# A decode block on one core: the last 20 row chunks of the down projection in seven loads instead of nine

## The chip, the cores and the metric

The kernel runs on one core of one Trainium2 chip. The metric is the device time of one execution in microseconds (us). A core has a matrix engine (PE, with its weight loads shown as PEld), three further engines for element work (DVE, ACT, POOL), and an engine SP that here only issues transfers. The transfers themselves run on 16 DMA engines that all issuers share; loads issued by SP queue up behind one another and are worked off in order.

## The reference

One token for each of 8 sequences goes through an attention block with a cached window and then a gated feed-forward block, all in float32:

```
h  = x + A(layernorm(x))        # q = x@wq; softmax over the last 1024 cached keys; 32 query heads on 4 kv heads; @wo
g  = layernorm(h) @ w_gate      # 1024 x 3584
u  = layernorm(h) @ w_up        # 1024 x 3584
h2 = h + (gelu(g) * u) @ w_down # 3584 x 1024
```

The activations are tiny (8 rows of 1024). The weights and the cache window are about 111 MB, and each byte is used once.

## The kernel before

All weights pass through two buffers in on-chip memory, `wbuf[0]` and `wbuf[1]`, of 64 KB on each of 128 partitions, 8 MB each. Twelve "units" of 8 MB are loaded in turn, unit 2k into buffer 0 and unit 2k+1 into buffer 1: wq, the keys, the values, wo, then gate and up (two units each). Each unit is one load of 128 rows (one row for each partition) of 64 KB. A load into a buffer waits until PE has finished with what lay there before, so SP issues it while the other buffer is still being filled.

PE works a unit off in one call of `half(i, gates)`: eight steps c = 0 to 7 of four matmuls each (each matmul is a group of 32 output partitions by 512 columns, float32, and appears as two records in the trace, so a step is eight records and a whole half 64). Steps 0 to 3 collect in one part of the PSUM tile `sums[i]`, steps 4 to 7 in the other. PE runs a loop of eight turns; a turn does the b half of one unit, a small summing matmul `y` (line 235), eight transposes (line 240) that turn activations into stationary operands, and then the a half of the next unit. A `gate` is a semaphore that PE waits on ahead of a step, and takes down again by the same amount.

The down projection is 28 row chunks of 128 rows by 1024 columns (512 KB each, 4 KB for each partition). Chunks 0 to 7 ride in the last two units, beside gate and up columns. The last 20 chunks are the end of the program:

- chunks 8 to 23 go into buffer 0 as the loads `wd0` ... (sizes in chunks: `PARTS`), issued as soon as PE has finished the last gate unit there. They are worked off by the last call of `half(0, ...)`, two chunks for each step.
- chunks 24, 25 and 26 go into buffer 1 as the loads `we0` ... (sizes: `ENDPARTS`), issued as soon as PE has finished the last up unit. Each is worked off by `chunk(q)`: four matmuls of 256 columns into the PSUM tile `acc` (line 428).
- chunk 27 comes in two column blocks, `wl0` of 160 and `wl1` of 96 columns for each of four groups (`ENDS`), worked off by four matmuls each (line 453).

Between these lies the fold: DVE adds up what the halves left (`d`, lines 422 and 423; the second add waits for the last matmul of the last `half(0)`), and four matmuls with the constant `add2` bring it into `acc` as well. ACT copies `acc` to `most`, DVE adds each column block of chunk 27 to it, and two stores send the result out.

All loads of weights are issued by SP in program order through one helper, line 93, each with a semaphore that reaches 16 when the load has landed. The gates of the last `half(0)`: ahead of step 0 it waits for `wd0` together with a signal of DVE that the stationary operand for steps 0 to 3 stands; ahead of later steps it waits for the later `wd` loads, and for DVE's signal that the operand for steps 4 to 7 stands (`go_later[0]`, line 408). Since the same loop body serves all turns, POOL gives these gates their amounts for the six earlier turns at the start of the program (line 196).

Of the kernel before, what the change touches and what calls it, by code (L numbers as in the profile page):

```python
# [16 lines left out]
QW = D // NQ  # L17
# [9 lines left out]
UNITS = 12  # L27
EARLY = 8
HEAD = 16
PARTS = (8, 4, 2, 2)  # L30
ENDPARTS = (1, 1, 1)
ENDS = (160, 96)
AHEAD = 3


GATE = (17, 16, 16)
TURNS = 9
NO_B = (1, 4)
NO_A = (3,)
# [2 lines left out]
class Flow:  # L42
# [37 lines left out]
    def run(self, engine, make, *waits, mark=True, gives=None):  # L80
        ins = self.start(engine, make, waits)
        if gives is not None:
            ins.then_inc(*gives)
            return None
        if not mark:
            return None
        self.done[engine] += 1
        ins.then_inc(self.own[engine], 1)
        return self.own[engine], self.done[engine]

    def move(self, name, out, src, *waits, engine="sync", sem=None):
        s = self.sem(name) if sem is None else sem
        self.start(engine, lambda e: e.dma_start(out, src), waits).then_inc(s, 16)  # L93
        return s, 16


def decode_block(nc, x, units, dn, tails, ends, outs):

    fl = Flow(nc)
# [4 lines left out]
    def sb(name, *shape):  # L104
        return nc.alloc_sbuf_tensor(name, list(shape), F32).ap()
# [10 lines left out]
    source = sb("source", P, 2 * N)  # L116

    go = [fl.sem("go_a"), fl.sem("go_b")]
    go_later = [fl.sem(f"go_{i}") for i in range(1, len(PARTS))]
    go_turn, go_fold = fl.sem("go_turn"), fl.sem("go_fold")  # L120


# [17 lines left out]
    def half_a(k, h=1):  # L140
        return at_mark["a", k, h]

    def half_b(k, h=1):
        return at_mark["b", k, h]
# [5 lines left out]
    for u in range(UNITS):  # L150
        k, i = divmod(u, 2)
# [4 lines left out]


    q0 = EARLY
    for i, (n, sem) in enumerate(zip(PARTS, (go[0], *go_later))):
        c0 = (q0 - EARLY) * D  # L160
        move(f"wd{i}", wbuf[0][:, c0:c0 + n * D], dn[i], half_a(passes - 2), sem=sem)
        q0 += n
    assert q0 == EARLY + HEAD
    arrived = {}
    c0 = 0
    for i, n in enumerate(ENDPARTS):
        here = move(f"we{i}", wbuf[1][:, c0:c0 + n * D], tails[i], half_b(nb - 1))
# [4 lines left out]
    last = q0  # L172
# [18 lines left out]
    add2 = sb("add2", P, 2, 32)  # L191
# [3 lines left out]
    for i, g in enumerate(go_later):  # L195
        run("gpsimd", lambda e: e.memset(note[:, i:i + 1], 0.0), gives=(g, GATE[i] * (passes - 1)))

# [10 lines left out]
    def take(sem, n):  # L208
        PE.wait_ge(sem, n).then_inc(sem, -n)  # L209

    def mark(ins):
        ins.then_inc(fl.own["tensor"], 1)

    def half(i, gates):
        gates = dict(gates)
        for c in range(NC):
            if c in gates:
                take(*gates[c])
            h = c // (NC // 2)
            for j in range(NQ):  # L220
                s = NQ * c + j
                ins = PE.matmul(  # L222
                    sums[i][32 * j:32 * j + 32, h * N:(h + 1) * N], still[i][:, 32 * s:32 * s + 32],
                    wbuf[i][:, s * N:(s + 1) * N],
                    start=(c % (NC // 2) == 0), stop=(c % (NC // 2) == NC // 2 - 1))
            if c % (NC // 2) == NC // 2 - 1:
                mark(ins)

    with nc.Fori(1, TURNS, engines=[mybir.EngineType.PE], hint_back_edge=True) as i:
        with PE.If(i != NO_B[0]):  # L230
            with PE.If(i != NO_B[1]):
                half(1, [(0, (go[1], 17))])
                take(go_fold, 1)
                for ch in range(2):
                    ins = PE.matmul(turned[0:32, ch * N:(ch + 1) * N], add2[:, ch, :], y_sb,  # L235
                                    start=True, stop=True)
                mark(ins)
        take(go_turn, 1)
        for n in range(NC):
            ins = PE.transpose(turned[:, n * P:(n + 1) * P], source[:, n * P:(n + 1) * P], ident)  # L240
        mark(ins)
        with PE.If(i != NO_A[0]):
            half(0, [(0, (go[0], 17)), *zip((4, 6, 7), zip(go_later, GATE))])
    fl.done["tensor"] = len(seq)


# [174 lines left out]
    d1 = sb("d1", P, N)  # L421
    tok = run("vector", lambda e: e.tensor_add(d1, rest, sums[0][:, 0:N]), tok, half_a(6, 0))
    d1_ok = run("vector", lambda e: e.tensor_add(d1, d1, sums[0][:, N:2 * N]), tok, half_a(6))


    def quarters(lhs, rhs, *waits, start=False, stop=False):
        for j in range(NQ):
            tok = run("tensor", lambda e: e.matmul(
                acc[32 * j:32 * j + 32, 0:QW], lhs(j), rhs(j), start=start, stop=stop),
                *waits, mark=(stop and j == NQ - 1))  # L430
        return tok

    def chunk(q, **flags):
        t, here = arrived[q]
        return quarters(lambda j: at[:, q, :], lambda j: t[:, j * QW:(j + 1) * QW], here, at_ok, **flags)

    chunk(last - 3, start=True)
    quarters(lambda j: add2[:, j // 2, :], lambda j: d1[:, (j % 2) * QW:(j % 2) * QW + QW], d1_ok)
    chunk(last - 2)
    tok = chunk(last - 1, stop=True)  # L440
    most = sb("most", P, QW)
# [9 lines left out]
    for (c0, n, t, here), d_ps in zip(blocks, (fin, sums[1])):  # L451
        for j in range(NQ):
            tok = run("tensor", lambda e: e.matmul(  # L453
                d_ps[32 * j:32 * j + 32, 0:n], at[:, last, :], t[:, j * n:(j + 1) * n],
                start=True, stop=True), here, d1_ok, mark=(j == NQ - 1))
# [100 lines left out]
```

## Time and profile before

| | |
|---|---|
| time, median of 3 runs | 263.91 us (263.86 to 264.18) |
| profiled execution: its own time | 264.18 us |
| its span, first to last instruction | 262.9 us |
| HBM read | 111.18 MB, 423 GB/s over the span |
| share of the span: PE, PEld, DVE, ACT, POOL | 54%, 17%, 17%, 5%, 3% |
| share of 16 DMA engines' span taken by SP's and the stores' packets | 98.4% |
| granted PE clock, mean | 0.79 of full speed |

The span leaves out 1.28 us of the profiled execution's time. Times within the span count from its start. In rows of the timeline the columns are start, duration from the first start to the last end, engine, line, operation, output and input tile, shape and count; in brackets stands how long the engine sat idle before, and what ended that. In rows of windows, the columns are the window, its length, each engine's busy time with its instructions, the granted clock, the DMA share and GB/s. In the windows a packet is counted where it is recorded, so that a window of 1 us can show a DMA share over 1 or zero while 64 KB rows are under way.

### The profile page before, as it was taken

To read this page: it belongs to the slowest core of one execution; us is meant where nothing else is said; L and a number is where in the kernel's file an instruction comes from. 1 tells how busy PE (TensorE), PEld (TensorE's weight loads), DVE (VectorE), ACT (ScalarE), POOL (GpSimd) and SP (SyncE) were. 2 spreads that over 40 slices of the span, in tenths; PEclk is the share of its full clock that TensorE was granted. 3 is DMA by queue.
4 is the path that set the end of the run, shared out by engine and by line. 5 is a ranking of instruction groups with operands and counts; after the bars stand their busy time and mean duration, and the time that the engine had idled before them with its cause. 6 is when DMAs were issued, how large, how long until landed. Compare 5 with 4: busy or idle time off the path is not lost. (4 is left out here: it accounts for less than half of the span.)

```text
span 262.9 us, 2262 instructions
## 1 busy us (share of the span) xinstructions
PE 141.5 (54%) x968; PEld 44.5 (17%) x968; DVE 43.8 (17%) x115; ACT 13.5 (5%) x19; POOL 7.2 (3%) x18
## 2 busy tenths in 40 slices
PE   0025706926807927608908409728509709319985
PEld 0021201211202312102302102122103202002321
DVE  0340200240100140400410100254100300100432
ACT  1000000000030010000000200000300000200000
POOL 5000100100000000100100000000000000000000
PEclk9999975985966965975976956965957957956999
DMA  8997997999799899979979997997997999799996
GB/s 319 484 459 339 479 479 339 459 479 479 319 479 479 349 449 479 479 319 479 479 329 469 479 469 329 479 479 319 479 479 319 479 479 479 319 479 399 400 421 239
DMA packets 3329, 111.33 MB, mean 424 GB/s; under 512 B 504, under 2 KB 760, under 8 KB 1280
## 3 DMA queue, kind: packets, MB, share of 16 engines
q1 hardware_dynamic: 3168, 111.23, 98.4%
q10 hardware_dynamic: 160, 0.08, 0.1%
q8 instruction: 1, 0.02, 0.0%
HBM read 111.18 MB, written 0.13 MB: 423 GB/s over the span
## 5 line engine op out<-in xcount | busy, mean ns | idle before, releaser
L222 PE MATMUL sum<-w,still 128*32 128x512 f32 x832 | 117.2, 726 | 96.3 <-PEq L209 96.3
L222 PEld LDWEIGHTS sum<-w,still 128*32 128x32 f32 x832 | 32.2, 130 | 177.1 <-issue 177.1
L240 PE MATMUL turned<-ident,source 128*128 128x128 f32 x64 | 11.0, 328 | 21.1 <-PEq L209 21.0
L240 PEld LDWEIGHTS turned<-ident,source 128*128 128x128 f32 x64 | 8.7, 167 | 26.4 <-issue 26.4
L235 PE MATMUL turned<-y_sb,add 128*32 128x512 f32 x24 | 11.3, 592 | 0.9 <-PEq L209 0.9
L318 DVE TENSOR_REDUCE nmax<-sum 128x1 f32<-128x1024 f32 x2 | 2.4, 1223 | 28.4 <-PE sum L222 28.4
L393 DVE TENSOR_TENSOR up<-up,sum 128x512 f32<-128x512 f32 (+1 forms) x2 | 1.4, 686 | 34.3 <-PE sum L222 34.3
L289 DVE TENSOR_SCALAR q<-sum 128x512 f32<-128x512 f32 x2 | 1.4, 692 | 25.2 <-PE sum L222 25.2
L274 DVE COPY still<-turned 128x1024 f32<-128x1024 f32 x4 | 4.7, 1219 | 4.2 <-PE turned L240 4.2
L383 DVE TENSOR_TENSOR gate<-gate,sum 128x512 f32<-128x512 f32 (+1 forms) x2 | 1.4, 685 | 23.6 <-PE sum L222 23.6
L345 DVE SCALAR_TENSOR_TENSOR o<-sum,share,o 128x128 f32<-128x128 f32 x12 | 4.2, 351 | 4.2 <-PE sum L222 3.8
L342 DVE TENSOR_SCALAR o<-sum,share 128x128 f32<-128x128 f32 x2 | 0.7, 350 | 24.0 <-PE sum L222 24.0
L320 ACT ACT_TABLE_LOAD x1 | 1.3, 1283 | 60.2 <-DVE nmax L318 60.2
L235 PEld LDWEIGHTS turned<-y_sb,add 128*32 128x32 f32 x24 | 2.6, 110 | 8.7 <-issue 8.7
L349 POOL MEMSET still<- 128x1024 f32 x2 | 1.9, 951 | 76.0 <-PE sum L222 76.0
L362 DVE TENSOR_TENSOR y_sb<-y_sb,sum 128x512 f32<-128x512 f32 x1 | 0.7, 686 | 15.8 <-PE sum L222 15.8
L294 POOL MEMSET still<- 128x1024 f32 x2 | 1.9, 957 | 46.5 <-PE sum L222 46.5
L360 ACT COPY y_sb<-sum 128x512 f32<-128x512 f32 x1 | 0.6, 586 | 50.7 <-PE sum L222 50.7
L320 ACT ACTIVATE source<-sum,nmax 128x1024 f32<-128x1024 f32 x2 | 2.2, 1113 | 17.1 <-PE turned L240 17.1
L361 DVE TENSOR_TENSOR y_sb<-y_sb,sum 128x512 f32<-128x512 f32 x1 | 0.7, 686 | 14.3 <-PE sum L222 14.3
L305 DVE COPY still<-turned 128x16 f32<-128x16 f32 x32 | 2.7, 161 | 2.1 <-PE turned L240 2.1
L382 ACT COPY gate<-sum 128x512 f32<-128x512 f32 (+1 forms) x2 | 1.2, 584 | 30.4 <-PE sum L222 30.4
(61 smaller groups left out, 40.3 us busy)
## 6 DMA issues: line engine op xcount, KB each, us to landing
w<-dn SPq DMA_DIRECT2D x1, 4096.0 KB, 19.8
w<-dn SPq DMA_DIRECT2D x1, 2048.0 KB, 24.3
w<-dn SPq DMA_DIRECT2D x2, 1024.0 KB, 27.3
w<-tails SPq DMA_DIRECT2D x3, 512.0 KB, 12.0
w<-ends SPq DMA_DIRECT2D x1, 320.0 KB, 13.1
w<-units SPq DMA_DIRECT2D x12, 29.4
w<-ends SPq DMA_DIRECT2D x1, 192.0 KB, 13.1
out<-o_fin SPq DMA_DIRECT2D x1, 80.0 KB, 1.6
```

The source lines that it names most:

```text
L222: ins = PE.matmul(sums[i][32 * j:32 * j + 32, h * N:(h + 1) * N], still[i][:, 32 * s:32 * s + 32], wbuf[i][:, s * N:(s + 1) * N], start=(c ...
L235: ins = PE.matmul(turned[0:32, ch * N:(ch + 1) * N], add2[:, ch, :], y_sb, start=True, stop=True)
L240: ins = PE.transpose(turned[:, n * P:(n + 1) * P], source[:, n * P:(n + 1) * P], ident)
L274: run("vector", lambda e: e.tensor_copy(still[i].rearrange("p (c j m) -> p c j m", c=NC, j=NQ), turned.rearrange("p (c m) -> p c m", c=NC) ...
L289: tok = run("vector", lambda e: e.tensor_scalar(q_sb, sums[hf][:, 0:N], scale, None, op0=ALU.mult), done(0, 0))
L294: cleared.append(run("gpsimd", lambda e: e.memset(still[hf], 0.0), done(0)))
L305: run("vector", lambda e: e.tensor_copy(to[:, :, b, s, a, REP * b:REP * b + REP].rearrange("p k (h i) -> p k h i", h=2), frm[:, s, a * HB ...
L318: tok = run("vector", lambda e: e.tensor_reduce(out=nmax, in_=sums[hf], axis=AX.X, op=ALU.max, negate=True), done(1))
L320: p_ok = run("scalar", lambda e: e.activation(source, sums[hf], AF.Exp, bias=nmax, accum_out=tot), tok, at_mark["t", 1 + hf])
L345: tok = run("vector", lambda e: e.scalar_tensor_tensor(out, o3[:, b], share[hf][:, b:b + 1], o_sb, op0=ALU.mult, op1=ALU.add), tok, done(2 ...
L349: cleared[hf] = run("gpsimd", lambda e: e.memset(still[hf], 0.0), done(2))
L383: tok = run("vector", lambda e: e.tensor_add(gate[:rows], gate[:rows], sums[0][:rows, N:2 * N]), tok, half_a(4 + k))
```

## The change

Two tables of sizes change, and with them the loads. Chunks 8 to 23 come as 10, 4 and 2 chunks in three loads instead of 8, 4, 2 and 2 in four. Chunks 24 to 26 come as 2 and 1 chunks in two loads instead of three of one chunk. The two column blocks of chunk 27 are as before. The number of bytes and their order are the same.

The gates of `half(0)` follow: the wait on DVE's signal for steps 4 to 7 stands alone now (amount 1 instead of 17, since no load ends at that step), the second load is waited for ahead of step 5, and the third ahead of step 7. At the end, the fold's four matmuls go ahead of those of chunk 24 and open the accumulation in `acc`.

```diff
-PARTS = (8, 4, 2, 2)
-ENDPARTS = (1, 1, 1)
+PARTS = (10, 4, 2)
+ENDPARTS = (2, 1)
 ENDS = (160, 96)
...
-GATE = (17, 16, 16)
+GATE = (1, 16, 16)
...
-    go_later = [fl.sem(f"go_{i}") for i in range(1, len(PARTS))]
+    go_later = [fl.sem(f"go_{i}") for i in range(len(GATE))]
...
-    for i, (n, sem) in enumerate(zip(PARTS, (go[0], *go_later))):
+    for i, (n, sem) in enumerate(zip(PARTS, (go[0], *go_later[1:]))):
...
-            half(0, [(0, (go[0], 17)), *zip((4, 6, 7), zip(go_later, GATE))])
+            half(0, [(0, (go[0], 17)), *zip((4, 5, 7), zip(go_later, GATE))])
...
-    chunk(last - 3, start=True)
-    quarters(lambda j: add2[:, j // 2, :], lambda j: d1[:, (j % 2) * QW:(j % 2) * QW + QW], d1_ok)
+    quarters(lambda j: add2[:, j // 2, :], lambda j: d1[:, (j % 2) * QW:(j % 2) * QW + QW], d1_ok,
+             start=True)
+    chunk(last - 3)
     chunk(last - 2)
     tok = chunk(last - 1, stop=True)
```

On SP, which issues the loads, the end of the program is this (`dn` is the source of chunks 8 to 23, `tails` of chunks 24 to 26, `ends` of chunk 27; the shape is partitions by float32 elements; `tensor_done` counts PE's finished halves):

```order
-L93 DMA w<-dn 128x8192 [waits tensor_done]
+L93 DMA w<-dn 128x10240 [waits tensor_done]
 L93 DMA w<-dn 128x4096
-L93 DMA w<-dn 128x2048 x2
-L93 DMA w<-tails 128x1024 [waits tensor_done]
-L93 DMA w<-tails 128x1024 x2
+L93 DMA w<-dn 128x2048
+L93 DMA w<-tails 128x2048 [waits tensor_done]
+L93 DMA w<-tails 128x1024
 L93 DMA w<-ends 128x640
 L93 DMA w<-ends 128x384
```

Four loads of `dn` have become three and three of `tails` two; the waits ahead of the first of each are the same.

On PE, in the loop's `half(0)`, a step of four matmuls is what stands between two gates or a multiple of it (`go_a` is the gate of step 0; in the program before `go_1` to `go_3` are the later ones, in the changed one `go_0` to `go_2`):

```order
 L222 MATMUL sum<-w,still 32x512 [waits go_a_done]
 L222 MATMUL sum<-w,still 32x512 x15
+L222 MATMUL sum<-w,still 32x512 [waits go_0_done]
+L222 MATMUL sum<-w,still 32x512 x3
 L222 MATMUL sum<-w,still 32x512 [waits go_1_done]
 L222 MATMUL sum<-w,still 32x512 x7
 L222 MATMUL sum<-w,still 32x512 [waits go_2_done]
 L222 MATMUL sum<-w,still 32x512 x3
-L222 MATMUL sum<-w,still 32x512 [waits go_3_done]
-L222 MATMUL sum<-w,still 32x512 x3
```

Gates stood ahead of steps 0, 4, 6 and 7; now they stand ahead of 0, 4, 5 and 7.

Behind the loop PE does the end of the down projection (`vector_done` is DVE's count, for the fold the second add of `d`; `we0_done` and so on are the landings of the loads of chunks 24 to 26):

```order
-L428 MATMUL acc<-w,at 32x256 [waits we0_done,vector_done]
-L428 MATMUL acc<-w,at 32x256 x3
 L428 MATMUL acc<-d,add 32x256 [waits vector_done]
 L428 MATMUL acc<-d,add 32x256 x3
+L428 MATMUL acc<-w,at 32x256 [waits we0_done]
+L428 MATMUL acc<-w,at 32x256 x7
 L428 MATMUL acc<-w,at 32x256 [waits we1_done]
 L428 MATMUL acc<-w,at 32x256 x3
-L428 MATMUL acc<-w,at 32x256 [waits we2_done]
-L428 MATMUL acc<-w,at 32x256 x3
```

The four matmuls of chunk 24 have moved from ahead of the fold to behind it, where they wait for the same load as those of chunk 25.

## The prediction

> **What bounds the kernel now.** I read the shares of the DMA queues first, since 111 MB for 8 tokens suggests a stream of weights.
>
> ```profile
> q1 hardware_dynamic: 3168, 111.23, 98.4%
> HBM read 111.18 MB, written 0.13 MB: 423 GB/s over the span
> ```
>
> The queue with the weights keeps the 16 DMA engines busy for 98.4% of the span, against 54% for PE: the stream of loads is the bound, and anything else counts only where the stream is held up or after it has ended. The chain of waits shows whether the end agrees (start, duration, what):
>
> ```profile
> 246.89 13.12 DMA w<-ends
> 260.01 0.04 issue
> 260.05 0.48 PE fin L453 x8
> 260.53 0.01 issue
> 260.54 0.42 PE sum L453 x8
> 260.96 0.02 issue
> 260.98 0.25 DVE o_fin L456
> ```
>
> The end hangs on the first column block `wl0`, which lands at 260.01 though it was issued 13.12 us earlier. It has been queuing. So the question is when the queue in front of it is empty; what follows its landing is the same in both kernels. For the pace of the queue I read PE's timeline, where a half starts when its load has landed:
>
> ```profile
> 22.68 8.71 PE L222 MATMUL sum<-w,still 128*32 128x512 f32 x64 [6.51 <-PEq L209]
> ...
> 207.32 1.09 PE L240 MATMUL turned<-ident,source 128*128 128x128 f32 x8
> 216.52 9.07 PE L222 MATMUL sum<-w,still 128*32 128x512 f32 x64 [8.11 <-PEq L209]
> 235.89 9.62 PE L222 MATMUL sum<-w,still 128*32 128x512 f32 x64 [10.30 <-PEq L209]
> 245.32 1.88 PE L235 MATMUL turned<-y_sb,add 128*32 128x512 f32 x4
> 247.13 1.09 PE L240 MATMUL turned<-ident,source 128*128 128x128 f32 x8
> 248.16 6.21 PE L222 MATMUL sum<-w,still 128*32 128x512 f32 x56
> 255.47 1.07 PE L222 MATMUL sum<-w,still 128*32 128x512 f32 x8 [1.10 <-PEq L209]
> 256.75 0.64 PE L428 MATMUL acc<-w,at 128*32 128x256 f32 x8 [0.21 <-DMA w<-tails]
> 257.34 0.64 PE L428 MATMUL acc<-d,add 128*32 128x256 f32 x8
> 257.94 0.64 PE L428 MATMUL acc<-w,at 128*32 128x256 f32 x8
> 259.21 0.64 PE L428 MATMUL acc<-w,at 128*32 128x256 f32 x8 [0.63 <-DMA w<-tails]
> 260.05 0.48 PE L453 MATMUL fin<-w,at 128*32 128x160 f32 x8 [0.20 <-DMA w<-ends]
> ```
>
> From 22.68 to 235.89 lie eleven units of 8 MB: 213.21 / 11 = 19.38 us for each, or 1.211 us for one chunk of 512 KB when sixteen come in one load. The last twenty chunks follow without a gap: step 7 of the last half waits (1.10 us) for the last `dn` load, chunks 24 and 26 wait for theirs, and the block waits for its own. PE is ahead of the stream by little, but ahead.
>
> **The change part by part.** *Two loads fewer.* What one load costs beyond its bytes I take from the stretch in which loads are small. From 235.89 (unit 11 has landed) to 260.05 (`wl0` has) is 24.16 us. In it came 16 + 3 + 0.625 = 19.625 chunks; at 1.211 us that is 23.77 us. The rest, 0.39 us, is the price of cutting: eight loads instead of the 19.625 / 16 = 1.2 which the rate already holds, so 6.8 extra loads at 0.057 us. Pieces of the stretch give the same size: the four `dn` loads took 255.47 - 235.89 = 19.58 us against 19.38 for one load of the same size, 0.20 us for three extra loads, 0.07 each; the loads of chunks 24 to 26 took (259.21 - 255.47) / 3 = 1.247 us each, 0.036 above 1.211. Two loads fewer at 0.057 are **0.115 us less**, of which one load lies in `dn` (0.057) and one in `tails` (0.058). The bounds: nothing, if the price belongs to the size of the rows alone and longer rows gain nothing here, and 0.39 us, if all of the loss went. Nothing excludes a small loss from a row of 40 KB, which the trace does not have; it has 64 KB rows and the 32 KB rows of `wd0` on both sides of it:
>
> ```profile
> 20.00:39.00 19.00, 8.71 (x64) 2.38 (x64) 1.38 (x2) 0.00 (x0) 0.96 (x1) 0.93 1.00 435
> 235.86:245.50 9.64, 9.61 (x65) 2.87 (x66) 0.00 (x0) 0.58 (x1) 0.00 (x0) 0.73 0.98 423
> 253.00:255.40 2.40, 1.37 (x16) 0.22 (x8) 0.00 (x0) 0.00 (x0) 0.00 (x0) 1.00 0.97 401
> 255.50:259.00 3.50, 2.87 (x32) 0.63 (x32) 0.69 (x1) 0.00 (x0) 0.00 (x0) 1.00 1.01 401
> ```
>
> The last two numbers of a row are the DMA share and GB/s: 435 with 64 KB rows, 423 with 32 KB rows (and an edge packet in or out), 401 with rows of 8 KB and of 4 KB. A ten-chunk load that ran like the smallest rows would take 10 x 0.036 = 0.36 us more; I take nothing, since both neighbours in size run well, and keep +0.25 us (0.36 less the 0.115) as the bad end.
>
> *Two issues fewer on SP.* Each takes about 0.43 us of SP:
>
> ```profile
> 225.65 1.77 SPq L93 DMA_DIRECT2D w<-dn  x4
> 245.57 1.28 SPq L93 DMA_DIRECT2D w<-tails  x3
> 246.89 0.91 SPq L93 DMA_DIRECT2D w<-ends  x2
> ```
>
> The `dn` issues at 225.65 come 10.2 us ahead of the end of unit 11's load at 235.89, and the last `ends` issue is over at 247.80 while the queue holds `dn` until 255.4. That stream hides them; the gain is nothing. Without that cover the two would be worth 0.86 us.
>
> *The ten-chunk load.* It lands two chunks later than the eight-chunk load did: 235.89 + 10 x 1.211 + 0.06 = 248.06. PE could not start the last half before the transposes end (247.13 + 1.09 = 248.22), and it started at 248.16 without waiting, so the later landing hides behind them, by 0.1 to 0.2 us. If it were late, step 0 would be late by as much. That still costs nothing for 1 us: steps 0 to 6 take 6.21 us and step 7 waits until 255.4.
>
> *Gates at 4, 5 and 7.* Steps 0 to 4 take 5 x 0.89 = 4.4 us (6.21 / 7 for a step) and end at 252.6. Step 5 now waits for the four-chunk load, the 14th chunk: 235.89 + 14 x 1.211 + 0.1 = 252.9, a wait of about 0.4 us that was not there. Steps 5 and 6 end at 252.9 + 1.77 = 254.7. Step 7 waits for the 16th chunk as before, now at 255.47 - 0.06 = 255.41: the new wait is eaten by 0.7 us that PE would have stood there anyway. The gate at step 4 needs only DVE's operand, and the row of DVE shows it ready at 249.3, ahead of 251.7 when step 4 is due.
>
> ```profile
> 248.86 0.43 DVE L408 COPY still<-at 128x512 f32<-128x512 f32 x1
> 256.59 0.69 DVE L423 TENSOR_TENSOR d<-d,sum 128x512 f32<-128x512 f32 x1 [4.04 <-PE sum L222]
> 259.92 0.37 ACT L442 COPY most<-acc 128x256 f32<-128x256 f32 x1 [17.19 <-PE acc L428]
> ```
>
> *The fold ahead of chunk 24.* The second add of `d` cannot start before step 7 is done; fold follows the landing of chunk 23 by 257.34 - 255.47 = 1.87 us, so it now starts at 255.41 + 1.87 = 257.28. While PE waits for it, 0.8 us, chunk 24 is queued behind, and its four matmuls (257.34 - 256.75 = 0.59 us) are no longer done in that gap. They go behind the fold: fold 257.28 to 257.88, chunk 24 to 258.48, chunk 25 to 259.08. The two-chunk load lands at 257.94 - 0.115 = 257.82 at the latest, behind which PE has no wait left. Chunk 26 lands at 259.21 - 0.115 = 259.10: PE arrives there 0.02 us before it. Chunk 26 ends at 259.70, `wl0` lands at 260.01 - 0.115 = 259.90. PE so loses the 0.6 us which it had and keeps 0.2 us of slack ahead of the block. ACT's copy of `acc` (0.37 us) ends near 260.1, ahead of the first add, which waits for PE until 260.5. The cost is nothing as long as fold starts before 259.90 - 4 x 0.60 = 257.50; from there on the end moves with it, one for one.
>
> *Sum:* 264.18 (the profiled execution) - 0.115 = 264.06. The median of the runs shown is 263.91, so the forecast is 263.91 - 0.115 = **263.8 us**.
>
> **The rivals.**
>
> *Faster: a load holds the queue for its landing time.* Loads would then not overlap their completion with the next one's bytes. The row for the store of 80 KB,
>
> ```profile
> w<-tails SPq DMA_DIRECT2D x3, 512.0 KB, 12.0
> out<-o_fin SPq DMA_DIRECT2D x1, 80.0 KB, 1.6
> ```
>
> has 1.6 us from issue to landing on an empty queue; 80 KB at 1.211 us for 512 KB is 0.2, so 1.4 us are fixed. Two loads fewer would give 2.8 us: 261.1 us. Against it: chunks 24 to 26 followed each other in 1.247 us, which leaves 0.04 us for anything fixed. The Trainium skill, "DMA: Bandwidth & Descriptors", section "Anatomy of one DMA — SWDGE (gpsimd) path", gives about 2.0 us fixed for each DMA beside bytes at 436 GB/s, measured on another issuing path than this, and its "Rules for kernel authors" ask for 1 MiB or more in a DMA. By that figure applied to each queued load, the estimate would be 4 us less, 259.9 us; the trace does not agree, since 512 KB loads queued behind each other took 1.247 us each. I give the rival 2%.
>
> *No gain at all.* The price of the small loads may lie in what is left small (`wl0`, `wl1`, chunk 26), or PE's chain of fold and three chunks takes over at the end. Both give 263.9. For it: PE's slack falls to 0.2 us. 12%.
>
> *Slower: PE's clock.* The granted clock falls to half after PE has been idle. If the new gaps (0.4 us ahead of step 5, 0.7 ahead of step 7, 0.8 ahead of the fold) did that, the end would be PE's. At half clock the same count of records takes twice as long:
>
> ```profile
> 236.00:239.00 3.00, 3.00 (x16) 0.77 (x19) 0.00 (x0) 0.00 (x0) 0.00 (x0) 0.50 1.21 524
> 241.00:244.00 3.00, 3.00 (x32) 1.00 (x28) 0.00 (x0) 0.58 (x1) 0.00 (x0) 0.99 1.21 524
> ```
>
> Fold and three chunks would take 4 x 0.60 more, the blocks 0.48 + 0.42 more, step 7 0.89 more; less the 0.2 us of slack that is 4.0 us: 267.8 us. It decides from the point at which one gap is long enough. Against it: in the rows
>
> ```profile
> 210.00:211.00 1.00, 0.00 (x0) 0.00 (x0) 0.00 (x0) 0.00 (x0) 0.00 (x0) 0.68 0.30 131
> 230.00:231.00 1.00, 0.00 (x0) 0.00 (x0) 0.00 (x0) 0.00 (x0) 0.00 (x0) 0.92 2.42 1049
> ```
>
> the clock (third number from the right) falls inside these windows, after PE had been idle from 208.4 and from 225.5, so after 2 and 5 us, and the gap of 1.10 us ahead of step 7 did not bring it down. 4%.
>
> *The ten-chunk row runs badly.* With the bad end above, 264.15 us; to be slower by more than what can be told it would have to run 5% below its neighbours. 5%.
>
> **How the numbers follow.** The forecast has 74%, no gain 12%, the bad row 5%, the clock 4%, the held queue 2%; 3% is left for what I have not seen, on both sides alike. About 0.2%, 0.5 us, is what a measurement of this kernel can tell from no change. The forecast's own bounds, a gain of 0 to 0.39 us, reach from 263.5 to 263.9; the runs before spread by 0.3 us, and the bad row adds 0.25 above, so the range is 263.4 to 264.2. The held queue (2%), half of the unseen (1.5%) and the error of the two timings beside a gain near its upper bound (2.5%) make faster 6%; the clock (4%), the other half of the unseen and a little of the bad row make slower 6%; same is 88%.
>
> **What would show it.** Right, if the gap between the landing of unit 11 and the start of `fin` shrinks from 24.16 us to about 24.05; if PE's last half has a new gap of about 0.4 us ahead of step 5 and starts step 7 within 0.1 us of 255.4; if fold, chunk 24 and chunk 25 run without a gap from about 257.3 to 259.1; and if the end still hangs on `ends`, with PE idle ahead of it. Wrong, if the chain of waits at the end goes through fold or chunk 26 instead of the column block, if the clock is below 1 after 250 us, if step 0 waits visibly for the ten-chunk load, or if the loads of 10 and 2 chunks take more than 1.211 us for each chunk by over 0.04.

## The result: slower by 0.45%, and the profile after

The changed kernel takes 265.20 us (median of 6 runs, 264.85 to 265.56), the kernel before 264.03 (6 runs, 263.86 to 264.32): a ratio of 1.0045, 95% interval 1.0035 to 1.0055, so 1.2 us more. The forecast was 263.8 us, within a range of 263.4 to 264.2. The profiled execution has 265.15 us and a span of 263.8, against 264.18 and 262.9.

PE's timeline of the changed kernel from the landing of unit 11 on:

```profile
235.77 9.53 PE L222 MATMUL sum<-w,still 128*32 128x512 f32 x64 [10.39 <-PEq L209]
...
247.94 4.50 PE L222 MATMUL sum<-w,still 128*32 128x512 f32 x40
252.79 1.92 PE L222 MATMUL sum<-w,still 128*32 128x512 f32 x16 [0.36 <-PEq L209]
255.28 1.06 PE L222 MATMUL sum<-w,still 128*32 128x512 f32 x8 [0.57 <-PEq L209]
257.15 0.64 PE L428 MATMUL acc<-d,add 128*32 128x256 f32 x8 [0.80 <-DVE d L423]
257.67 1.07 PE L428 MATMUL acc<-w,at 128*32 128x256 f32 x16
258.94 0.64 PE L428 MATMUL acc<-w,at 128*32 128x256 f32 x8 [0.20 <-DMA w<-tails]
259.79 0.48 PE L454 MATMUL fin<-w,at 128*32 128x160 f32 x8 [0.21 <-DMA w<-ends]
261.53 0.37 PE L454 MATMUL sum<-w,at 128*32 128x96 f32 x8 [1.26 <-DMA w<-ends]
```

Up to the row of `fin` the forecast holds: from 235.77 to 259.79 are 24.02 us, where before it was 24.16 and 24.05 was expected. Then PE waits 1.26 us more for the last load, `wl1`, 192 KB. In the kernel before its four matmuls followed those of `wl0` without a wait (260.05, 260.54). The chain of waits says the same; its end now hangs on the second column block:

```profile
246.68 14.81 DMA w<-ends
261.49 0.04 issue
261.53 0.42 PE sum L454 x8
261.95 0.02 issue
261.97 0.26 DVE o_fin L457
```

What became of these 1.26 us is in the windows of the changed kernel (DMA share and GB/s are the last two numbers):

```profile
259.00:259.50 0.50, 0.50 (x8) 0.10 (x8) 0.12 (x3) 0.00 (x0) 0.00 (x0) 1.00 1.06 371
259.50:260.00 0.50, 0.29 (x12) 0.16 (x8) 0.00 (x0) 0.35 (x1) 0.00 (x0) 1.00 0.09 28
260.00:260.50 0.50, 0.27 (x8) 0.00 (x0) 0.16 (x1) 0.02 (x1) 0.00 (x0) 1.00 0.07 9
260.50:261.00 0.50, 0.00 (x0) 0.00 (x0) 0.16 (x1) 0.00 (x0) 0.00 (x0) 1.00 0.06 12
```

From 260.0 to 261.0 the DMA share is 0.06 to 0.07. One engine of 16 is 0.0625: fifteen are done, and one is still at work on `wl1`. What held it up stands in the table of DMA queues, taken for short windows. First the changed kernel, 259.0 to 259.2 (packets, MB, share of 16 engines; a packet is counted where it starts):

```profile
q1 hardware_dynamic: 50, 0.07, 91.1%
q8 instruction: 1, 0.02, 33.9%
```

and then the kernel before, 259.8 to 260.0:

```profile
q8 instruction: 1, 0.02, 34.5%
q1 hardware_dynamic: 29, 0.02, 34.2%
```

It is a fetch of 16 KB of program code, one packet on one engine: 33.9% of 16 engines for 0.2 us are 1.09 us. In the kernel before it starts at 259.85, at the moment at which an engine ends its part of `wl1`. In the changed kernel it starts at 259.06, and seven of one engine's eight packets of `wl1` are late: in the record of packets seven of 1.5 KB start between 260.13 and 260.98, the first five taking 0.15 to 0.19 us each instead of 0.065. The record names no engine; that they are on the engine of the fetch is taken from the first of them starting within 0.02 us of the fetch's end (259.06 + 1.09 = 260.15). A load has landed when all 16 engines have marked it. Fifteen marks of `wl1` were there by 260.23, the sixteenth at 261.49.

### The profile page after: what moved, and what is told of

Its sections match the earlier page's. It is cut to its first block, busy times and chain, and to the rows that moved or that the text cites. A ratio compares the mean times of both kernels' runs of the same rounds, so it can differ in the third digit from the quotient of the medians.

```text
span 263.8 us, 2259 instructions
## 1 busy us (share of the span) xinstructions
PE 139.6 (53%) x968; PEld 44.2 (17%) x968; DVE 43.8 (17%) x115; ACT 13.5 (5%) x19; POOL 7.2 (3%) x18
## 5 line engine op out<-in xcount | busy, mean ns | idle before, releaser
L222 PE MATMUL sum<-w,still 128*32 128x512 f32 x832 | 115.4, 715 | 97.8 <-PEq L209 97.8
```

The lines of the kernel that those rows point to most:

```text
L222: ins = PE.matmul(sums[i][32 * j:32 * j + 32, h * N:(h + 1) * N], still[i][:, 32 * s:32 * s + 32], wbuf[i][:, s * N:(s + 1) * N], start=(c ...
```

## Experiments

Theories at the start: F, the fetch is set off by DVE as it passes three small memsets of tile `ahead` behind the load of chunk 26 (they run at 259.02, 0.04 us ahead of the packet); P, it belongs to PE; L, the last load is late for its own sake.

**The wait of the memsets moved (`e1_late_fetch`, `e2_before_early`).**

```diff
 # e1, in the changed kernel            # e2, in the kernel before
-    ... arrived[last - 1][1], d1_ok)
+    ... blocks[0][3], d1_ok)            # e1: wait for wl0
+    ... arrived[last - 2][1], d1_ok)    # e2: wait for the load of chunk 25
```

> The changed kernel, with one wait moved: the three small DVE memsets of tile ahead wait for the landing of wl0 instead of the load of chunk 26, about 0.8 us later. Theory F (DVE, when it passes these memsets, sets off a fetch of 16 KB of instructions, and the fetch cuts in on one DMA engine ahead of that engine's part of wl1): the instruction packet starts behind the last packet of wl1, at about 259.8 to 260.0 instead of 259.06; wl1 lands within 0.5 us of wl0; time 263.8 (the forecast of the change), 1.3 us under the changed kernel. Rival P (the fetch belongs to PE's code, whose length the change altered, and has nothing to do with ahead): the packet stays at 259.06 and the time at 265.2. Rival L (the last load is late for a reason of its own, its size and place in the shorter queue, and the fetch is an accident beside it): wl1 still lands 1.7 us after wl0, time 265.2, wherever the packet is.

> The kernel before, with the memsets of tile ahead waiting for the load of chunk 25 instead of chunk 26, 1.27 us earlier. Theory F: the instruction packet moves from 259.85 to about 258.5 and cuts in on one engine ahead of its parts of both column blocks; both land about 1.1 us late, time 265.0. Rival P and rival L: nothing moves, 263.9 to 264.1.

Measured: e1 265.28 us (4 runs, 265.14 to 265.69; ratio 1.0051, 1.0034 to 1.0067), e2 264.02 (one run). In e1 the memsets run 0.6 us later, and the packet does not follow them:

```profile
258.71 0.64 PE L428 MATMUL acc<-w,at 128*32 128x256 f32 x8 [0.21 <-DMA w<-tails]
259.54 0.48 PE L454 MATMUL fin<-w,at 128*32 128x160 f32 x8 [0.19 <-DMA w<-ends]
261.32 0.44 PE L454 MATMUL sum<-w,at 128*32 128x96 f32 x8 [1.30 <-DMA w<-ends]
```

These are PE's rows of e1's timeline; DVE's row of the memsets in it is

```profile
259.61 0.12 DVE L448 MEMSET ahead<- 1x1 f32 x3 [2.78 <-DMA w<-ends]
```

The packet starts at 258.84, ahead of them. In e2 the memsets run at 257.90 and the packet starts at 259.38, at its engine's end. Theory F falls.

**The change taken apart (`e3_parts`, `e4_tails`, `e5_fold`).**

```diff
 # e3: PARTS, GATE and the gates as changed; ENDPARTS = (1, 1, 1), fold behind chunk 24
 # e4: ENDPARTS = (2, 1); all else as before
 # e5: the fold ahead of chunk 24; all nine loads as before
```

> Only the loads of chunks 8 to 23 changed (10, 4, 2) with their gates; chunks 24 to 26 in three loads and the fold behind chunk 24 as before. Theory F in the form that the fetch only just misses or hits the boundary between the engine's parts of wl0 and wl1: the landing of chunk 26 and what queues behind it are as before, so the packet stays behind wl1, time 263.9 - 0.06 = 263.85. Rival P: PE has as many instructions as before in the last stage, 263.85 as well. Rival L (fewer loads in the queue make the last one late): part of the 1.2 us, 264.3 to 265.

> Only the loads of chunks 24 to 26 changed (2, 1), with the fold between chunks 24 and 25. Theory F: if the coarser load changes when the last of the three chunks is seen to land relative to the engine's part of wl0, the packet cuts in ahead of wl1 as in the changed kernel, 265.1; if not, 263.85. Rival P: PE has one waiting instruction fewer; if that is what moves the fetch, 265.1. Rival L: part of the 1.2 us, 264.3 to 265.

> The kernel before with one edit: the fold goes ahead of chunk 24; all nine loads as before. By then it was known that the fetch does not follow the DVE memsets, and that the loads alone, of either group, leave it behind wl1. Theory Q (the fetch is PE's: one waiting instruction fewer ahead of the chunks, which the fold's place brings with it, or the earlier issue of the chunks behind the fold, sets it off so early that the engine serves it between its parts of wl0 and wl1): the instruction packet cuts in ahead of wl1, wl1 lands 1.5 us or more behind wl0, time 265.0 to 265.3. Rival M (it takes the coarse loads and the fold's place together): the packet behind wl1, 264.0.

Measured, one run each: e3 263.76, e4 263.92, e5 265.07 us. In e3 and e4 the packet stands behind its engine's part of `wl1` (259.41, 259.28), in e5 it is in front again (259.09, five packets of `wl1` behind it). The place of the fold alone brings the late landing, with all nine loads. Rivals L and M fall by these profiles and not by the three times, which are single ones; e11 below shows that one kernel can give both. e5 also shows something else: PE at half clock, by its windows,

```profile
255.00:256.00 1.00, 0.79 (x8) 0.19 (x8) 0.00 (x0) 0.00 (x0) 0.00 (x0) 1.00 1.04 414
256.00:257.00 1.00, 0.27 (x4) 0.00 (x0) 0.67 (x1) 0.00 (x0) 0.00 (x0) 0.94 1.01 401
257.00:258.00 1.00, 0.93 (x12) 0.47 (x16) 0.02 (x1) 0.00 (x0) 0.00 (x0) 0.50 1.01 401
```

so that a chunk takes 0.86 us and `fin` starts at 260.40. That is not what ends this execution, since `wl1` lands later, at 261.40. The profiled execution of the changed kernel had full clock.

**Longer code on PE (`e6_pad1`, `e7_before_pad`, `e8_pad6`).** One waiting instruction on PE for something long done, ahead of fold (e6) or of chunk 24 (e7); six in e8.

```diff
+    for _ in range(1):          # e7: 3, which build as one more instruction; e8: 12, as six
+        PE.wait_ge(*at_ok)
```

> The changed kernel with one waiting instruction more on PE, ahead of the fold, for something that is long done, so that PE's code is as long as before. If it is the length of PE's code that counts (Q, length): the packet stands behind wl1 as before the change, time 263.8. If it is the order or the issue time of the chunks (Q, order), or rival M: 265.2 as in the changed kernel.

> The kernel before with one waiting instruction more on PE, ahead of chunk 24. Q, length: if shorter code is what brings the fetch forward, longer code leaves it behind wl1, 264.0; if any shift from the length of before does it, 265.2. Q, order and rival M: 264.0.

> The changed kernel with six waiting instructions more on PE ahead of the fold. If PE's place in its code sets off the fetch, it comes six instructions (one and a half matmuls of the chunks) earlier in the order of the chunks than in the run with one more: earlier in the stream, so that the packet cuts in on the load of chunk 26 or on wl0, 264.9 to 265.3. If not: 265.2 with the packet between wl0 and wl1 as in the changed kernel.

Measured: e6 265.14 us (10 runs, 264.15 to 265.50; ratio 1.0038, 1.0024 to 1.0051), e7 264.06, e8 265.18 (one run each). Neither the length of the code nor its shift by six instructions decides it. In e6's profile the packet starts at 259.26, when its engine has done all its packets of `wl1` and not yet written its mark; the mark alone is late, lands at 261.45, and the time is that of the others. How much of `wl1` is behind the packet hardly matters; that anything is, costs 1.2 us. One reason shows in the records: in the changed kernel the last mark counts 0.45 us after its packet starts, and the other fifteen about 0.5; in e6, where it follows the fetch directly, it is 1.10 us.

**The waiting that holds PE (`e9_hold`, `e10_swap`).** A helper of the kernel turns several waits into waiting instructions that stand alone, but for the last, which rides on the instruction itself. In the kernel before, chunk 24 waits for its load and for DVE's operand; the wait for the load stands alone, as the first thing PE meets behind its loop. It is one row in the profile before (the waits of line 74 on PE's sequencer):

```profile
L74 PEldq EVENT_SEMAPHORE  x1: 51/51/51, 256.6 to 256.6; - x1
```

It is passed at 256.64, and the profile after has no such row: the fold waits for one thing, which rides on its weight load, and chunk 24 then has only its load to wait for.

```diff
 # e9, in the changed kernel, ahead of the fold
+    PE.wait_ge(*d1_ok)
 # e10, in the kernel before, in chunk(): the same two waits in the other order
-    ..., here, at_ok, **flags)
+    ..., at_ok, here, **flags)
```

> The changed kernel with one waiting instruction on PE ahead of the fold, for the second add of d, on which the fold waits anyway. Theory G (PE's sequencer asks for the next 16 KB of its code as soon as it runs on behind the loop; a waiting instruction that stands alone holds it, a wait that rides on a weight load does not; asked for at 255.4 the fetch comes out about 3.7 us later, ahead of the end of its engine's part of wl1, asked for later it finds that engine done): held until about 257.1, the packet stands behind its engine's last packet, wl1 lands 0.5 us behind wl0, time 263.8. Rival O (it is the order of fold and chunks, or the issue of the chunks in one go, whatever the waiting): 265.1, as with the waiting instruction for something long done.

> The kernel before with the two waits of chunk 24 exchanged: the one for DVE's operand, long done, stands alone, and the one for the load rides on the weight load. Same instructions, same loads, same order. Theory G: nothing holds PE's sequencer behind the loop any more, the packet comes at about 255.5 + 3.7 = 259.2, ahead of its engine's last packets of wl1, wl1 lands over 1 us late, time 265.1. Rival O: 264.0, as before.

Measured: e9 **263.89 us** (11 runs, 263.74 to 264.24; ratio 0.9995, 0.9986 to 1.0003), e10 **265.33 us** (3 runs, 265.18 to 265.96; ratio 1.0055, 1.0041 to 1.0070). Both as theory G has it, and rival O falls. e9 and e6 have the same instructions in the same order; the instruction that waits alone is passed at 257.19 in e9 and at 255.48 in e6. In e9 the packet starts at 259.66, no packet of `wl1` is late (the last starts at 259.77), and `wl1` lands at 260.32, 0.49 us behind `wl0`. e9's end:

```profile
257.30 0.64 PE L428 MATMUL acc<-d,add 128*32 128x256 f32 x8 [0.89 <-DVE d L423]
257.74 1.07 PE L428 MATMUL acc<-w,at 128*32 128x256 f32 x16
259.04 0.64 PE L428 MATMUL acc<-w,at 128*32 128x256 f32 x8 [0.23 <-DMA w<-tails]
259.88 0.48 PE L455 MATMUL fin<-w,at 128*32 128x160 f32 x8 [0.20 <-DMA w<-ends]
260.36 0.37 PE L455 MATMUL sum<-w,at 128*32 128x96 f32 x8
```

and e10's, which differs from the kernel before in nothing but which of two waits stands alone:

```profile
256.39 0.64 PE L428 MATMUL acc<-w,at 128*32 128x256 f32 x8
257.08 0.64 PE L428 MATMUL acc<-d,add 128*32 128x256 f32 x8
257.68 0.64 PE L428 MATMUL acc<-w,at 128*32 128x256 f32 x8
258.96 0.64 PE L428 MATMUL acc<-w,at 128*32 128x256 f32 x8 [0.65 <-DMA w<-tails]
259.79 0.48 PE L453 MATMUL fin<-w,at 128*32 128x160 f32 x8 [0.19 <-DMA w<-ends]
261.57 0.37 PE L453 MATMUL sum<-w,at 128*32 128x96 f32 x8 [1.30 <-DMA w<-ends]
```

Its waiting instruction is passed at 255.49, the packet starts at 259.21, and `wl1` lands at 261.53.

**The loads without the fold, and a later hold (`e11_loads`, `e12_hold_load`).**

```diff
 # e11: the change, with the fold between chunks 24 and 25 as before
 # e12, in the changed kernel, ahead of the fold
+    PE.wait_ge(*arrived[last - 3][1])    # the load of chunks 24 and 25
```

> The change without the move of the fold: seven loads, with the fold between chunks 24 and 25 as before. Theory G: chunk 24's waiting instruction for its load stands alone and holds PE until about 257.6, the packet behind wl1; the two loads saved show alone: 264.0 - 0.115 = 263.9, with a stretch from the landing of unit 11 to that of wl0 of 24.05 us. Rival O: the same. If the coarse loads were part of the harm: 264.3 to 265.

> The changed kernel with one waiting instruction on PE ahead of the fold, as in the run that held it until the second add of d, but for the landing of the load of chunks 24 and 25, so that PE is held until about 257.65 instead of 257.19. The run of the loads alone, held to the same time with the old order of fold and chunks, had two kinds of executions, seven near 263.9 and five near 265.2. Theory G with a latest time (a request as late as 257.65 can again meet the engine before it is done): executions of both kinds here too. If G has no such limit and the mixture came from the old order: all near 263.9. The fold starts 0.4 us later, which leaves PE about even with the landing of wl0; up to 0.1 us of cost.

Measured: e11 264.03 us (12 runs, 263.71 to 265.38; ratio 1.0017, 1.0003 to 1.0032), of which seven took 263.71 to 264.04 and five 265.06 to 265.38; e12 263.94 (12 runs, 263.71 to 265.28; ratio 1.0001, 0.9987 to 1.0015), with two at 265.07 and 265.28. Both release PE at 257.6 to 257.7. So holding PE longer is not safer: executions of both kinds come back, with either order. Five against two of twelve is no difference that twelve runs can tell. The profiled executions of both took less than 264.8 us, so that those near 265.2 have the same cause is taken from their times alone. The table has what is known of the hold, by the time from the landing of unit 11 to the last wait that stands alone, with how many times of each kernel lie over 264.8 us. Where the packet stands is from one profile of each kernel:

| kernel | fold | PE released after | packet against its engine's end | times over 264.8 us |
|---|---|---|---|---|
| changed, e1, e5 | first | nothing holds it | ahead | 6 of 6, 4 of 4, 1 of 1 |
| e6 | first | 19.8 | ahead | 9 of 10 |
| e10 | second | 19.9 | ahead | 3 of 3 |
| e8 | first | 20.5 | ahead | 1 of 1 |
| e3 | second | 20.7 | behind | 0 of 1 |
| before, e2, e7 | second | 20.8 | behind | 2 of 66, 0 of 1, 0 of 1 |
| e9 | first | 21.3 | behind | 0 of 11 |
| e4, e11, e12 | second, second, first | 21.9 | behind | 0 of 1, 5 of 12, 2 of 12 |

**Seven loads, by themselves.** The stretch from unit 11 to `fin` in the profiles: nine loads 24.16 us (before), 24.18 (e2) and 24.17 (e10); eight 24.07 (e3); seven 24.02 (changed), 24.02 (e1), 24.01 (e6) and 24.03 (e9). It is 0.14 us less with seven loads, whatever becomes of `wl1` behind it.

## Why the prediction was wrong, step by step

**What failed** is the sentence under the chain of waits: "what follows its landing is the same in both kernels". It let the account stop at the landing of `wl0`, and took for granted that `wl1` lands 0.5 us behind. The term left out of the sum is the one packet of code, whose row stood on the page of before:

```profile
q8 instruction: 1, 0.02, 0.0%
```

I read the row of the weights' queue beside it and did not ask when that packet ran. At 259.85 it starts just where the stream of loads ends, and that nearness was the warning: where it came 0.6 to 1.0 us earlier (259.26 in e6 to 258.84 in e1), it fell on the last load, at +1.2 us. None of the rivals had it. The clearest place to see what the change would do to it was in the instructions themselves: the first wait behind PE's loop goes from two semaphores to one, so that a waiting instruction which stands alone disappears. I costed edits by instructions added and moved, and this one is a wait dropped.

**The two loads fewer.** Forecast 0.115 us, measured 0.14 in the stretch to `fin`; with the late landing taken away (e9) the time is 263.89 against 264.03, 0.14 us less, though the interval of the ratio (0.9986 to 1.0003) does not tell that from nothing. The size was right. The sum put the price on the load and kept the size of the rows as a bound; the records of packets, one for each row, put most of it on the rows. A row of 40 KB takes 1.514 us, one of 32 KB and one of 8 KB together 1.525; a row of 8 KB takes 0.314, two of 4 KB about 0.320. An engine has eight rows of each load, so the two merges save about 0.09 and 0.05 us, and two marks of 0.009 us besides: 0.16 us by this estimate. On this queue the price of a load was 0.07 us (0.14 / 2), and a load that held the queue for its landing, the rival worked out as 2.8 us, is out. The Trainium skill's fixed 2.0 us for a DMA ("DMA: Bandwidth & Descriptors", section "Anatomy of one DMA — SWDGE (gpsimd) path"), given there for another issuing path, would have made it 4 us, an estimate that these runs do not bear out.

**The gates.** Step 5 waits 0.36 us (forecast 0.4), step 7 starts at 255.28 (255.41) and waits 0.57 (0.7). The ten-chunk load does not show in the changed kernel: step 0 starts at 247.94 without a wait. In e8, e11 and e12, where PE came to step 0 earlier, it did wait for that load, 0.54 to 0.95 us, until 12.11 or 12.12 us after unit 11: 1.21 us for each chunk, as with rows of 64 KB. All of it is hidden, as forecast, and the row of 40 KB costs nothing.

**The fold.** It starts 1.87 us behind step 7 (257.15 - 255.28), as forecast; fold and chunks follow each other, in 0.52 to 0.54 us each and not 0.60; PE is 0.21 us ahead of `wl0` (0.2 forecast). "The cost is nothing" was right for PE's own time, and it was the move that cost 1.2 us through a thing that was not on PE's timeline.

**The clock.** Not what made the changed kernel slow: 1.00 at its end. But e5's row shows that the clock can fall there, in the second of two gaps of 1.43 and 0.80 us, and at half clock a chunk took 0.86 us and not the 1.2 that I had priced. The length of one gap does not decide it: e10 had a gap of 1.43 us at the same place, and its windows from 255 to 261 have 1.00.

**What is shown and what is argued.** Shown: one 16 KB packet of code ahead of an engine's last packet or mark of `wl1` goes with a sixteenth mark 1.2 to 1.3 us behind the fifteenth, in six profiles of six (in the eight others it comes at most 0.20 us behind); an instruction on PE that waits alone, and how long, decides which it is (e6 against e9; before against e10), and neither the order of fold and chunks nor the length of the code does. Argued: that PE's sequencer asks for the code as soon as it runs on behind the loop. No row names the owner of the fetch, but only edits on PE moved it across its engine's part of `wl1`. Open: why a request from 255.5 comes out 3.7 to 3.8 us later (e6, e10) and ahead of its engine's end, one from 256.6 or 257.2 behind it, and one from 257.6 either way. e8 fits least: its six short waits end at 256.24 and the packet comes 3.0 us later, ahead; in e3 the hold ends at 256.25 and the packet stands behind.

## What to carry to other kernels

In a kernel that ends on its last loads, look up every packet that is not a load, by queue and by time: here a single fetch of code on one of 16 engines delayed a load by more than its own length (1.09 us of fetch, 1.2 us in the time). Where a wait goes away, ask what it held back besides the instruction behind it. If the only cost of a hold is time in which the engine would wait anyway, as in e9, it is a way to place such a fetch; but its window here was narrow on both sides, so it has to be timed over many executions and not judged by a median alone (e11's and e12's medians, 264.03 and 263.94, hide times of 265.1 to 265.4).

## What was not expected of the hardware

- Code is fetched through the same 16 DMA engines as data: 16 KB, one packet, 1.08 to 1.10 us on one engine in every profile here, against 0.065 us for a packet of 1.5 KB. The first five packets behind it took 0.15 to 0.19 us each.
- Which of two waits of one instruction stands alone is worth 1.3 us (e10), with the same instructions, loads and order.
- The same program has executions 1.2 us apart: e11 seven of 12 near 263.9 us and five near 265.2, the kernel before two of 66 over 264.8.
- The granted clock fell to half within 2 us of a gap of 1.43 us in e5, where the same gap in e10 left it at 1.00.
